# Loading the first four chunks of an attention stage as two pairs

## The chip, the cores and the metric

The kernel runs on one core of a Trainium2 chip. Its time is the device time in microseconds (us) of one execution; lower is better. Before the change five executions took 206.04 to 207.04 us, with a median of 206.45 us. One more execution was recorded by the hardware profiler. It took 206.08 us, of which the recorded span, from the first instruction to the last, is 204.3 us; the other 1.8 us lie around the span.

The engines carry their profile names: PE is the matrix engine (PEld its loading of weights into the array), DVE the vector engine, ACT the scalar engine, POOL the GpSimd engine, and SP the engine whose queue issues most of the transfers. A q behind a name (SPq, POOLq) means that engine's queue.

## The reference

A gated linear attention is followed by a two-layer network with an exact GELU. For each of 4 batches and 8 heads, a 48x48 state decays by a gate and takes up an outer product at each of 768 positions:

```python
f = 1.0 / (1.0 + np.exp(-f_logit))
for t in range(S):
    state = f[:, :, t, :, None] * state + np.einsum('bhd,bhe->bhde', k[:, :, t], v[:, :, t])
    y[:, :, t] = np.einsum('bhd,bhde->bhe', q[:, :, t], state)
```

The result is brought into the form x = 3072 positions x 384 and goes through

```python
h = x @ w_in                                    # 384 x 2048
g = 0.5 * h * (1.0 + erf(h * inv_sqrt2))
return g @ w_out                                # 2048 x 384
```

All inputs are 32-bit floats. q, k, v and f_logit are laid out as batch, head, position, dimension: one position of one head is a run of 48 numbers, 192 bytes, and two neighbouring positions of a head are one run of 384 bytes.

## The kernel before

**The tiling.** The 3072 positions are 24 chunks of 128, six to a batch. A chunk passes an attention stage, which turns the recurrence into matrix products within the chunk and a state carried from chunk to chunk, and its result is copied, transposed, into a tile `xT`. Chunks form groups of 4, 2, 2, 4, 4, 4, 4 (`SIZES`, L187); when all of a group's chunks are in `xT`, the network runs on the group: `f1` (L511 to L516) multiplies by w_in, ACT applies the GELU (L519), `f2` (L530 to L533) multiplies by w_out, and a copy and a store finish each chunk.

**The attention stage of a chunk.** `chunk_in` (L315) loads its f_logit, k, q and v as four transfers on the SP queue, 192 KB each, one position per partition, so that each consists of 1024 runs of 192 bytes. `stage1` (L329) works on batches of chunks (`BATCH`, L199; one chunk at a time for the first six): exponential and logarithm on ACT (L336, L339) give the log of the gate; a product with a triangle of -1, `trin` (L349), gives running sums; two exponentials of these (`rg` L356, `gt` L352) are multiplied on DVE into the keys (`kp` L359) and the queries (`qp` L363); POOL casts the values into `vp` (L369); small products with `negcol` (L377) give the decay of the whole chunk, `gl`. `attn` (L393) transposes keys and queries (L406); copies out of the matrix memory put them into `kb`, a block form with zeros between the heads, and `qT`; products of both (L425) are masked on DVE to `am` (L429); the state is brought on (L441, L452 to L458, L464); `am` times `vp` (L477) and the old state times `qT` (L481) give the result, which a wide copy (L490) and three narrow ones (L494) bring into `xT`. All of these copies go through one helper (L219 on ACT, L221 on DVE).

**The order of the work.** Nothing is ordered at run time. A planner (`Plan`, L64 to L160) is given every operation with an engine, an estimated duration, a priority and what it depends on, places them all on estimated times, and the instructions are emitted engine by engine in that order. Each engine then executes its queue strictly in order. Some copies of the first `ALTN` chunks have a second engine among which the planner chooses; `BIAS` (L195) adds 0.8 us to the estimate wherever ACT is the alternative. `LOCK` (L192) says from which chunk on a group's first GELU and first `f1` product wait until the exponentials and running sums of the next chunks are done, so that ACT changes its function table less often.

**Loads and weights.** `ORDER` (L188) is the order in which transfers are planned: c for a chunk, W for half of w_in, O for a quarter of w_out. Weights are issued from the POOL queue, which casts them to 16 bits: `load_win` (L292) moves a half of w_in as six transfers, three of 96 rows and three of 32; `load_wout` (L297) a quarter of w_out as one. The planner's weights-first gate (L592 to L599) lets some f_logit loads wait on SP until an earlier weight has landed. While PE waits in the opening, it multiplies `trin` by itself (L587), for no result.

```python
SIZES = [4, 2, 2, 4, 4, 4, 4]
ORDER = ['c0', 'c1', 'c2', 'c3', 'O3', 'W0', 'W1', 'O1', 'c4', 'O0', 'O2']
BATCH = [1, 1, 1, 1, 1, 1, 2, 2, 2, 2, 2, 4, 2, 1, 1]
```

Of the kernel before, what the change touches and what calls it, by code (L numbers as in the profile page):

```python
# [15 lines left out]
class Ring:  # L16


    def __init__(self, bufs, make=None, fixed=None):
        self.bufs, self.make, self.fixed, self.order = bufs, make, fixed, []  # L20
# [5 lines left out]
class Buf:  # L26
# [3 lines left out]
    def ready(self):  # L30

        r = self.ring
        if self.slot is not None or len(r.order) < r.bufs:
            return 0.0
        old = r.order[len(r.order) - r.bufs]
        t = 0.0
        for u in old.users:
            if u.end is None:
                return None
            t = max(t, u.vis)  # L40
        return t
# [15 lines left out]
JITTER = 2.0  # L57


class Op:  # L60
    __slots__ = ("eng", "dur", "fn", "bufs", "prio", "deps", "table", "start", "end", "vis", "seq", "name", "alt", "nb")


class Plan:  # L64


    def __init__(self, seed=0, bias=0.0):
        self.ops, self.w, self.r = [], {}, {}
        self.rnd, self.bias = random.Random(seed) if seed else None, bias

    def add(self, eng, dur, fn, rd=(), wr=(), bufs=(), prio=0.0, deps=(), table=None, name="", alt=None):
        o = Op()
        o.alt, o.nb = alt, 0.0
        o.eng, o.dur, o.fn, o.bufs, o.prio, o.table, o.name = eng, dur, fn, tuple(bufs), prio, table, name
# [24 lines left out]
    def run(self):  # L99
        free = {e: 0.0 for e in LAT}  # L100
        if self.rnd:
            for o in self.ops:
                o.prio += self.rnd.uniform(-JITTER, JITTER)
        act = None
# [7 lines left out]
        while left:  # L112
            best, stay, cand = None, None, []
            for o in left:
# [10 lines left out]
                for eng, dur in ((o.eng, o.dur),) if not o.alt else ((o.eng, o.dur), o.alt):  # L125
# [7 lines left out]
            for t, o, eng, dur in cand:  # L133
                if o.table and act and o.table != act and stay is not None and stay < t + 2 * SWITCH:
                    continue
                key = (int((t + (self.bias if o.alt and eng == "ACT" else 0)) * 20 + 0.999), o.prio, o.seq, t + dur)
# [9 lines left out]
            o.vis = o.end + LAT[o.eng]  # L146
# [17 lines left out]
def kernel(  # L164
# [23 lines left out]
    ORDER = ['c0', 'c1', 'c2', 'c3', 'O3', 'W0', 'W1', 'O1', 'c4', 'O0', 'O2']  # L188
    EARLY = 1.5
    WARM, FILL = 26.0, 0.75  # L190
    RMAJOR = 0
    LOCK = 12  # L192
    KBALT = 1
    ALTN = 6
    BIAS = 0.8  # L195
    SEED = 0
    CRING = 1
    HPB, ASB = 3, 3
    BATCH = [1, 1, 1, 1, 1, 1, 2, 2, 2, 2, 2, 4, 2, 1, 1]  # L199
# [5 lines left out]
    ld = ctx.enter_context(tc.tile_pool(name="ld", bufs=8))  # L205
# [8 lines left out]

    P = Plan(SEED, BIAS)

# [10 lines left out]
    negcol = one.tile([C, 1], BF16, name="negcol")  # L227

# [4 lines left out]


    NLF, NQ = 2, 4
# [3 lines left out]
    vps = [one.tile([C, H * VB], BF16, name=f"vp{i}") for i in range(NQ)]  # L239
    kbs = [one.tile([C, P2, 2, C], BF16, name=f"kb{i}") for i in range(2)]  # L240
# [12 lines left out]

    P.add("POOL", 0.5, lambda: make_identity(nc, ident), wr=["ident"], prio=-90)
    P.add("POOL", 0.5, lambda: tri(trin, -1.0), wr=["trin"], prio=-100)
    P.add("POOL", 0.5, zpad(lfs[0]), wr=["lfz0"], prio=-99)
    P.add("DVE", 0.65, zall(vps[0]), wr=["vpz0"], prio=-99)
    P.add("POOL", 0.5, lambda: tri(mask, 1.0), wr=["mask"], prio=-80)
    P.add("POOL", 0.1, lambda: nc.gpsimd.memset(negcol, -1.0), wr=["negcol"], prio=-80)
    for i in range(NQ):  # L260
        P.add("POOL", 0.2, zpad(qps[i]), wr=[f"qpz{i}"], prio=-95 + 10 * i)
        P.add("POOL", 0.2, zpad(kps[i]), wr=[f"kpz{i}"], prio=-95 + 10 * i)
        if i:
            P.add("DVE", 0.65, zall(vps[i]), wr=[f"vpz{i}"], prio=-94 + 10 * i)
    for i in range(2):
        P.add("DVE", 0.5, zall(kbs[i]), wr=[f"kbz{i}"], prio=-93 + 10 * i)
        P.add("DVE", 0.3, zall(sbs[i]), wr=[f"sbz{i}"], prio=-92 + 10 * i)
        if i:
            P.add("POOL", 0.5, zpad(lfs[i]), wr=[f"lfz{i}"], prio=-60)
# [3 lines left out]
    r_in = {n: Ring(8, lambda n=n: ld.tile([C, H, D], F32, name=n)) for n in ("qt", "kt", "vt")}  # L273
    r_lf = Ring(NLF, fixed=lfs)
    r_qp, r_kp, r_vp = Ring(NQ, fixed=qps), Ring(NQ, fixed=kps), Ring(NQ, fixed=vps)
# [3 lines left out]
    r_kb, r_sb = Ring(2, fixed=kbs), Ring(2, fixed=sbs)  # L279
    r_qT = Ring(3, lambda: at.tile([C, P2, C], BF16, name="qT"))  # L280
    r_am = Ring(3, lambda: at.tile([C, 4, C], BF16, name="am"))
# [10 lines left out]
    def load_win(kk, half, ch):  # L292
        p0, p1, r0 = ((0, 96, 96 * kk), (96, 128, 288 + 32 * kk))[half]
        cs = slice(ch * d_ff // 2, (ch + 1) * d_ff // 2)
        return nc.gpsimd.dma_start(out=win[p0:p1, kk, cs], in_=moe_w_in[r0:r0 + p1 - p0, cs])
# [4 lines left out]

    G = [dict(xT=r_xT.new(), gT=r_gT.new()) for _ in range(NG)]
    E = [dict(fl=r_fl.new(), lf=r_lf.new(), gl=r_gl.new(), glp=(r_as if CRING else r_hp).new(), gate=[]) for _ in BATCH]
# [11 lines left out]

    def chunk_in(n, prio):  # L315
        g, j = bat[n]
        b, c = divmod(n, nC)

        def src(a):
            return a[b, :, c * C:(c + 1) * C, :].rearrange("h t d -> t h d")  # L320
        f = E[g]["fl"]
# [7 lines left out]
    def stage1(g):  # L329
# [4 lines left out]
        dl = 0.19 + 0.32 * s  # L334
        pr = 10 * efirst[g]
        P.add("ACT", dl, lambda: nc.scalar.activation(fl.t()[:, 0:s], fl.t()[:, 0:s], AF.Exp, scale=-1.0),  # L336
# [6 lines left out]
        for n in ns:  # L343
# [24 lines left out]
            def cast(x=x):  # L368
                nc.gpsimd.tensor_copy(x["vp"].t().rearrange("p (h x) -> p h x", x=VB)[:, :, 0:D], x["vt"].t())  # L369
# [23 lines left out]
    def attn(n):  # L393
# [94 lines left out]
        def cols():  # L488
            return slice(j * C, (j + 1) * C)
# [155 lines left out]
```

## Time and profile before

| what | value |
|---|---|
| median of five executions | 206.45 us (206.04 to 207.04) |
| profiled execution, and its span | 206.08 us, 204.3 us |
| first `f1` product starts | 28.74 us into the span |
| last product ends, last store is issued | 201.0 us, 201.52 us |
| busy shares: PE, PEld, DVE, ACT, POOL | 93%, 63%, 61%, 66%, 27% |
| moved by DMA | 27.02 MB; HBM read 25.17 MB, written 4.72 MB |
| loads of f_logit, k, q, v | 96 transfers of 192 KB |
| load queue (SP), weight queue (POOL) | 64.9% and 10.3% of 16 engines' span |

The first page of the profile also shows each engine's busy share in 40 equal slices of about 5.1 us, in tenths:

```profile
PE   6998769999889997997999999999999999999993
DVE  6599740039793899989998589963299862000000
```

A slice of PE marked 9 is not proof of a busy array: products overlap in the pipeline, and the opening's products on `trin` count as busy. In the DVE row the two zeros in the seventh and eighth slices are the time in which PE runs the first group's `f1`. The granted PE clock is in the top tenth in all 40 slices.

### The profile page before, as it was taken

The numbers are of one execution on the slowest core, as the hardware profiler recorded it, in microseconds if no ns is written. First come the engines' busy times: TensorE is split into PE (matmuls) and PEld (weight loads), VectorE is DVE, ScalarE is ACT, GpSimd is POOL, SyncE is SP. The second block draws the span as 40 slices with busy tenths as digits, with TensorE's granted clock in tenths as the row PEclk, the third lists the DMA queues.
The fourth block names the chain that finished last, engine by engine and source line by source line (L and its number), as shares of the span: only waits on it lengthen the run. The fifth ranks groups of instructions, "written<-read, shape, count | busy, mean of one in ns | idle before, by whom it ended". The sixth has DMA issues, their size and how long they took to land.

```text
span 204.3 us, 4585 instructions
## 1 busy us (share of the span) xinstructions
PE 189.6 (93%) x1746; PEld 128.1 (63%) x1746; DVE 124.1 (61%) x270; ACT 135.6 (66%) x247; POOL 54.6 (27%) x117
## 2 busy tenths in 40 slices
PE   6998769999889997997999999999999999999993
PEld 5888734456567766865666677655676655644561
DVE  6599740039793899989998589963299862000000
ACT  4445349964579597977968973878978773169410
POOL 7238990004024135312333032030042200000000
PEclk9999999999999999999999999999999999999999
DMA  7999999999999999998999999400121000220022
GB/s 130 187 177 162 180 161 174 187 198 247 205 201 187 172 229 192 171 196 197 203 187 169 188 177 242 97 0 2 42 77 39 3 0 0 80 77 0 0 77 77
DMA packets 106388, 27.02 MB, mean 132 GB/s; under 512 B 100480, under 2 KB 105600, under 8 KB 106368
## 3 DMA queue, kind: packets, MB, share of 16 engines
q1 hardware_dynamic: 103296, 23.60, 64.9%
q0 software_dynamic: 3072, 3.15, 10.3%
q8 instruction: 13, 0.21, 0.5%
q14 instruction: 7, 0.06, 0.1%
HBM read 25.17 MB, written 4.72 MB: 146 GB/s over the span
## 4 chain that ended last, share of the span: by engine, by line
PE 67%; DVE 10%; SPq 8%; DMA 6%; issue 4%; ACT 2%; POOL 1%; DVEq 0%; ACTq 0%; POOLq 0%
PE hps L532 26%; PE hps L515 24%; SPq L326 7%; PE aps L477 4%; DMA fl<-in_f_logit_dram 4%; PE tp L406 4%; PE aps L425 3%; DVE xT L221 3%; DVE am L429 3%; DMA vt<-in_v_dram 2%; PE aps L481 2%; DVE qp L363 2%; PE aps L441 1%; PE aps L349 1%; DVE kb L221 1%
## 5 line engine op out<-in xcount | busy, mean ns | idle before, releaser
L515 PE MATMUL hps<-xT,win 128*128 128x512 bf16 (+1 forms) x336 | 69.0, 349 | 1.9 <-DVE xT L221 1.7
L532 PE MATMUL hps<-wout,gT 128*128 128x384 bf16 x384 | 68.2, 326 | 0.0
L519 ACT ACTIVATE gT<-hps 128x512 bf16<-128x512 f32 x96 | 56.4, 597 | 12.8 <-PE hps L515 9.9
L532 PEld LDWEIGHTS <-gT 128*128 128x128 bf16 x384 | 36.4, 98 | 21.9
L515 PEld LDWEIGHTS <-win 128*128 128x128 bf16 x336 | 31.5, 98 | 25.7 <-issue 2.8
L221 DVE CAST xT<-aps 96x384 bf16<-96x384 f32 (+1 forms) x92 | 32.7, 355 | 9.2 <-PE aps L481 6.0
L429 DVE TENSOR_TENSOR am<-aps,mask 128x512 bf16<-128x512 f32 x48 | 31.0, 685 | 6.5 <-PE aps L425 6.1
L369 POOL CAST vp<-vt 128x384 bf16<-128x384 f32 x24 | 12.7, 529 | 62.4 <-DMA vt<-in_v_dram 37.7
L477 PE MATMUL aps<-am,vp 128*128 128x128 bf16 x192 | 19.8, 219 | 3.0 <-DVE am L429 2.6
L458 POOL TENSOR_TENSOR tn<-rr,gl 128x384 f32<-128x384 f32 x16 | 13.5, 845 | 29.6 <-DVE rr L456 23.3
L219 ACT ACTIVATE osb<-hps 128x384 f32<-128x384 f32 x18 | 8.8, 489 | 18.2 <-PE hps L532 18.0
L477 PEld LDWEIGHTS <-vp 128*128 128x128 bf16 x192 | 15.5, 98 | 8.6 <-issue 3.6
L359 DVE TENSOR_TENSOR kp<-kt,rg 128x384 bf16<-128x384 f32 x24 | 14.2, 590 | 10.5 <-ACT rg L356 10.2
L464 POOL CAST sb<-tn 48x192 bf16<-48x192 f32 x40 | 15.9, 397 | 12.3 <-PE aps L477 3.9
L221 DVE COPY kb<-tp 48x512 bf16<-48x512 bf16 x42 | 17.5, 418 | 0.6
L336 ACT ACTIVATE fl<-fl 128x384 f32<-128x384 f32 (+2 forms) x15 | 10.7, 715 | 10.1 <-DMA fl<-in_f_logit_dram 10.0
L356 ACT ACTIVATE rg<-aps 128x384 f32<-128x384 f32 x24 | 11.8, 491 | 7.3 <-PE aps L349 6.2
L604 ACT ACT_TABLE_LOAD x12 | 15.4, 1283 | 0.9 <-PEq L629 0.7
L587 PE MATMUL hps<-trin 128*128 128x128 bf16 x170 | 14.4, 247 | 1.4 <-POOL trin L231 1.4
L481 PE MATMUL aps<-qT,sb 128*128 128x128 bf16 x80 | 15.1, 219 | 0.0
L425 PE MATMUL aps<-qT,kb 128*128 128x128 bf16 x192 | 14.9, 219 | 0.0
L363 DVE TENSOR_TENSOR qp<-qt,gt 128x384 bf16<-128x384 f32 x24 | 14.7, 612 | 0.2
(42 smaller groups left out, 171.4 us busy)
## 6 DMA issues: line engine op xcount, KB each, us to landing
fl<-in_f_logit_dram SPq DMA_DIRECT2D x24, 192.0 KB, 4.5
kt<-in_k_dram SPq DMA_DIRECT2D x24, 192.0 KB, 4.4
qt<-in_q_dram SPq DMA_DIRECT2D x24, 192.0 KB, 4.5
vt<-in_v_dram SPq DMA_DIRECT2D x24, 192.0 KB, 4.4
out_dram<-osb SPq DMA_DIRECT2D x24, 192.0 KB, 2.1
wout<-in_moe_w_out_dram POOLq DMA_DIRECT2D x4, 384.0 KB, 7.7
win<-in_moe_w_in_dram POOLq DMA_DIRECT2D x6, 192.0 KB, 5.0
win<-in_moe_w_in_dram POOLq DMA_DIRECT2D x6, 64.0 KB, 4.4
```

Source lines behind the costliest of these rows:

```text
L221: nc.vector.tensor_copy(dst, src)
L363: P.add("DVE", 0.57, lambda x=x, gt=gt: nc.vector.tensor_tensor(x["qp"].t()[:, :, 0:D], x["qt"].t(), gt.t(), ALU.mult), rd=[("gt", n), ("q ...
L425: nc.tensor.matmul(ap_.t()[:, i * C:(i + 1) * C], kb.t()[:, p, hh, :], qT.t()[:, p, :], start=True, stop=True)
L429: P.add("DVE", 0.69, lambda ap_=ap_, am=am: nc.vector.tensor_tensor(am.t(), ap_.t().rearrange("p (h t) -> p h t", t=C), mask.unsqueeze(1). ...
L464: nc.gpsimd.tensor_copy(sb.t()[64 * hh:64 * hh + D, :, D * hh:D * hh + D], tn.t()[64 * hh:64 * hh + D, :, D * hh:D * hh + D])
L477: nc.tensor.matmul(yp.t()[:, p * C:(p + 1) * C], vwin(vp.t(), 2 * p + hh), ams[half].t()[:, 2 * (p % 2) + hh, :], start=(hh == 0), stop=(h ...
L481: nc.tensor.matmul(yp.t()[:, p * C:(p + 1) * C], osb.t()[:, p, :], qT.t()[:, p, :], start=False, stop=True)
L515: nc.tensor.matmul(hps.t()[:, i * tok:(i + 1) * tok], win[:, kk, fo * 128:(fo + 1) * 128], xT.t()[:, kk, 0:tok], start=(kk == 0), stop=(kk ...
L519: acts.append(P.add("ACT", 0.6, lambda u=u, hps=hps: nc.scalar.activation(view()[:, u * pk:(u + 1) * pk, :].rearrange("p a b -> p (a b)"), ...
L532: nc.tensor.matmul(op.t()[:, 0:d_model], view()[:, fo, s_ * C:(s_ + 1) * C], wout[:, fo, :], start=(fo == 0), stop=(fo == FO - 1))
L587: nc.tensor.matmul(buf.t()[:, 0:C], trin, trin, start=True, stop=True)
L604: nc.scalar.preload_act_table_set("natural_log_exp_and_others" if table == "exp" else "gelu_and_others")
```

## The change

The first four chunks (`2 * NDB`, NDB = 2) are loaded as pairs. Partition p holds positions 2p and 2p+1 of a 256-position pair, so that a pair's f_logit, k, q and v are four transfers of 384 KB, each of 1024 runs of 384 bytes. Within the pair a "chunk" becomes the even or the odd positions:

- running sums take two products each, with two new triangles (`trin2`), as do the sums for `gl` (`neg2`);
- the values are cast twice per chunk, each time one half of the partitions into a buffer whose other half stays zero, and `kb` is twice as wide with zero padding, so that the scores and results of each half come from two accumulated products per block; the mask is replaced by four half-wide pieces (`mask2`);
- the copies into `xT` put the positions back into order with a stride of two.

The pieces of w_in become quarters (`NW = 4`), each in two transfers of 96 and 32 partitions over all three blocks (before: halves in six transfers). A weight's issue on POOL now waits until a load `AHEAD = 4` transfers before it in the order has landed. The order of transfers, the batches, `LOCK`, `ALTN`, `BIAS` and the priorities (a table `PRI` in place of none) change, as do ring sizes: inputs 8 to 6 (plus 2 pairs), `vp` 4 to 6, `kb` 2 to 3, `am` 3 to 5. The diff, cut to its core:

```diff
-    ORDER = ['c0', 'c1', 'c2', 'c3', 'O3', 'W0', 'W1', 'O1', 'c4', 'O0', 'O2']
+    ORDER = ['c0', 'c1', 'W0', 'c2', 'c3', 'W1', 'c4', 'W2', 'c5', 'c6', 'W3', 'O0', 'O1', 'O2', 'O3']
+    AHEAD = 4
+    NW = 4
-    LOCK = 12
+    LOCK = 4
-    ALTN = 6
-    BIAS = 0.8
+    ALTN = 4
+    BIAS = 0
+    PRI = {'F': 2, 'RG': 5, 'R': -2, 'GL': 2, 'Tk': 20, 'VC': -10, 'Y': 20, 'x': 2, 'QT': 10, 'C': -2, 'T': 2, 'O': -20, 'A': 2}
+    NDB = 2
-    BATCH = [1, 1, 1, 1, 1, 1, 2, 2, 2, 2, 2, 4, 2, 1, 1]
+    BATCH = [2, 2, 1, 1, 2, 1, 1, 2, 4, 2, 1, 1, 2, 1, 1]
...
+    def tri_half(t, strict):
+        nc.gpsimd.memset(t, 0.0)
+        nc.gpsimd.affine_select(out=t, in_=t, compare_op=ALU.is_gt, fill=-1.0,
+                                base=strict, pattern=[[-1, C]], channel_multiplier=1)
+        nc.gpsimd.memset(t[0:64, 64:C], 0.0)
...
+    def load_win(half, ch):
+        p0, p1, r0 = ((0, 96, 0), (96, 128, 288))[half]
+        cs = slice(ch * d_ff // NW, (ch + 1) * d_ff // NW)
+        src = moe_w_in[r0:r0 + KO * (p1 - p0), cs].rearrange("(k p) c -> p k c", p=p1 - p0)
+        return nc.gpsimd.dma_start(out=win[p0:p1, :, cs], in_=src)
...
+            def src2(a):
+                return a[b, :, c * C:(c + 2) * C, :].rearrange("h (p i) d -> p h (i d)", i=2)
+            P.add("DMA", 1.35, lambda: nc.sync.dma_start(
+                out=pairs(f).rearrange("p (h x) -> p h x", h=H), in_=src2(f_logit)),
...
+            def cum(gps=gps, j=j):
+                for i in range(1 + dbl):
+                    nc.tensor.matmul(gps.t()[:, 0:H * D], trin2[:, int(i > j)] if dbl else trin,
+                                     lf.t()[:, i if dbl else j, :, 0:D], start=(i == 0), stop=(i == dbl))
...
+            for a, vb in enumerate(x["vp"]):
+                rows = slice(64 * a, 64 * a + 64) if dbl else slice(0, C)
+
+                def cast(vb=vb, rows=rows, n=n):
+                    nc.gpsimd.tensor_copy(vb.t()[rows].rearrange("p (h x) -> p h x", x=VB)[:, :, 0:D],
+                                          loaded(n, "vt")[rows])
...
+                    for e in range(4):
+                        p, hh = 2 * half + e // 2, e % 2
+                        for a in range(two):
+                            nc.tensor.matmul(ap_.t()[:, e * C:(e + 1) * C], kbv(kb, a)[:, p, hh, :],
+                                             qT.t()[:, p, :, 64 * a:64 * a + 64] if dbl else qT.t()[:, p, :],
+                                             start=(a == 0), stop=(a == two - 1))
...
+    def weight(i, dur, fn, name, wr):
+        dm = [o for o in P.ops if o.home == "DMA"]
+        gate = dm[-AHEAD] if len(dm) >= AHEAD else None
+
+        def issue():
+            made[name] = r = fn()
+            if gate is not None and gate.name in made and gate.name[0] == "l":
+                wait_for(r, gate.name)
```

## The prediction

> **What bounds the kernel now.** I first read the busy time of the engines in stages that I cut where the chain of waits changes character. The columns are the stage, its length, then busy time (and instructions) of PE, PEld, DVE, ACT, POOL, the granted clock, the DMA share and GB/s.
>
> ```profile
> 16.80:28.74 11.94, 8.68 (x146) 8.12 (x146) 9.42 (x21) 5.39 (x13) 11.75 (x23) 1.00 1.10 173
> 28.74:39.10 10.36, 10.36 (x49) 4.70 (x48) 0.27 (x1) 9.69 (x16) 1.51 (x3) 1.00 1.17 178
> 39.10:60.60 21.50, 19.60 (x185) 12.98 (x184) 14.55 (x31) 13.56 (x27) 4.62 (x9) 1.00 1.12 208
> 60.60:96.30 35.70, 32.60 (x360) 25.14 (x358) 30.40 (x66) 28.35 (x52) 11.69 (x22) 1.00 1.17 192
> 96.30:128.00 31.70, 31.70 (x308) 21.27 (x306) 27.25 (x60) 24.14 (x41) 9.59 (x19) 1.00 1.17 194
> ```
>
> PE looks full, but a busy PE is no measure. So I price its products by stretches in which they run back to back, from the chain of waits (start, length, what):
>
> ```profile
> 169.76 10.40 PE hps L532 x64
> 180.16 10.36 PE hps L515 x48
> ```
>
> That is 0.1625 us for an `f2` product and 0.216 for a 512-wide `f1` product; likewise 0.108 for a 256-wide one, 0.056 for the 128-wide ones of the attention stage, 0.16 for L349. With the counts of each stage:
>
> - 39.1 to 60.6: 64 `f2` (10.4), 20 narrow `f1` (2.2), 68 attention products (3.8), the small ones 1.6: 18.0 of 21.5, so 3.5 lost.
> - 60.6 to 96.2: 10.4 + 8.5 + 161 attention products (9.0) + 3.0: 30.9 of 35.6, 4.7 lost.
> - 96.2 to 201.1: 41.5 + 41.6 + 17.9 + 3.9 = 104.9 of 104.9. Nothing is lost.
>
> Hence span = **T** (start of the first `f1`, 28.74) + 164.2 of work + **S** (8.2 lost after T) + 3.3 of copy and last store. Before T only 7.8 us of PE work is useful. Only T and S can give anything.
>
> T is set by the loads. ACT's first exponential waits for f_logit in each of the first four chunks (start, length, engine, line, what, and in brackets the idle time before):
>
> ```profile
> 3.91 0.52 ACT L336 ACTIVATE fl<-fl 128x384 f32<-128x384 f32 x1 [1.90 <-DMA fl<-in_f_logit_dram]
> 8.10 0.52 ACT L336 ACTIVATE fl<-fl 128x384 f32<-128x384 f32 x1 [1.60 <-DMA fl<-in_f_logit_dram]
> 12.29 0.52 ACT L336 ACTIVATE fl<-fl 128x384 f32<-128x384 f32 x1 [1.53 <-DMA fl<-in_f_logit_dram]
> 16.83 0.52 ACT L336 ACTIVATE fl<-fl 128x384 f32<-128x384 f32 x1 [2.11 <-DMA fl<-in_f_logit_dram]
> ```
>
> 4.2 us a chunk, so 1.05 us per transfer of 1024 short runs; f1 then starts 11.9 us after the fourth f_logit. In that time DVE is busy for 9.42 of 11.94 us: it is the next bound.
>
> **The pair loads.** 16 transfers go, 8 of double size come. The trace has no 384-byte run. If only runs count, a pair costs 1.05; if bytes count, 2.10. The second is unlikely: weights read at twice the moved bytes (read as 32 bits, written as 16), 6.29 MB in 10.3% of 204.3 us, i.e. 21 us, or 300 GB/s against 187 here. Between these ends I take a rule of the Trainium skill, "DMA: Bandwidth & Descriptors", section "How a descriptor splits into AXI transactions": a run is fetched in 32-byte beats from the 256-byte boundary below it. At 192-byte steps the runs need 6, 12, 10 and 8 beats with the unused head, 9 on average; at 384 bytes 12 and 16, so 14. With the 3 cycles per packet that its section "Why small descriptors are slow" gives, 12 against 17: 1.05 x 17/12 = 1.49 us, an estimate. The page also speaks against the change: "Specifications" asks for at least 512 bytes for line rate, and 384 is still below. By that rule alone, priced by bytes, the sum is 8 x 2.1 = 16.8 us, no saving; by the estimate it is 11.9, **4.9 us saved** of DMA time. I take 1.5.
>
> **When things land.** First f_logit pair: 3.91 + 0.45 = 4.4. The first w_in quarter now goes between the pairs: a quarter is 1/8 of the 21 us, 2.6. Second f_logit pair: 4.4 + 4 x 1.5 + 2.6 = 13.0, against 16.83 for chunk 3. Then 17.5 for its last part, W1 20.1, c4 24.3, W2 26.9, c5 31.1, c6 35.3, W3 37.9, the four O at 40.5 to 48.3. Before, all weights and c4 to c6 were in when c6's values were cast at 51.94: 3.6 later.
>
> **The stage of the pairs.** Exponential and logarithm take 0.84 each for two chunks (row 128x768) instead of 4 x 0.52: first `kp` at 4.4 + 1.7 + 0.75 (two running-sum products) + 0.52 = 7.4, 1.3 later than now (6.08). Zeroing on DVE grows: `kb` 3 x 0.96 (0.272 for 256 words, 0.485 for 512, so 0.83 ns a word for 1088) and `vp` 6 x 0.485, 6.4 with `sb` against 3.45, all before 7.4 and hidden; uncovered it would cost 3.0. PE gains 32 score and 32 result products (3.6), and 1.8 of sums: 5.4 us, beside 14.4 us of idle products; without that cover 5.4. POOL: masks and paddings 7.2 against 4.4, four more casts (2.1), but by T only some six weight issues at 0.52 instead of 16 (9.5 us with w_out): 20 of 26 us busy, as now. A weight that waits for a load has casts and state copies queued behind it on POOL; their consumers (L441, L481) have slack of some us after the second pair's f_logit, so I cost that 0, at most 2. The casts collide with DVE. Here is one (now at chunk 3):
>
> ```profile
> 20.98 0.70 DVE L363 TENSOR_TENSOR qp<-qt,gt 128x384 bf16<-128x384 f32 x1
> 21.33 0.71 POOL L369 CAST vp<-vt 128x384 bf16<-128x384 f32 x1
> ```
>
> Alone they take 0.55 and 0.50: 0.15 each. The Trainium skill, "SBUF — State Buffer", section "Who interferes with whom", has the second one blocked entirely by the first when both read that memory: up to 0.5 each. Four more casts: 0.6 by the row, 2.1 by the rule; I take the row.
>
> DVE's work before T is 22.0 - 3.45 = 18.55 us, and it needs 22.7 us for it (82%). The number of operations stays. With `BIAS` 0 ACT takes more copies: bounds 0 and 5 us (ACT has about 10 of 22 us free); I take 2.5. 18.55 - 2.5 + 0.6 = 16.65: at 82% T = 7.4 + 20.3 = 27.7, at 95% 24.9. DVE waits for four loads now and for two then, so between: **T = 26.5, 2.2 earlier**. W0 has long landed.
>
> **After T.** `f1` of the first group has its first 12 units (7.8 us) by 34.3; W3 lands at 37.9. Chunk 4's attention (1.9) lies in the gap, 1.7 lost. `f2` needs the last O at 48.3, but `f1` of group 1 (5.2) and chunks 5, 6 (3.8) fill PE until then. The 3.5 lost there before (c4 came only after all weights) become 1.7. In 60 to 96 DVE is busy for 30.4 of 35.7: loads come 3.6 earlier, but DVE stays; 4.7 becomes 3.8. **S = 5.5, 2.7 less.** `LOCK` 4 holds group 3's `f1` until the exponentials of c12 to c15, one batch (1.48 twice): c15's f_logit is issued at 85.52 and lands about 90 now, 86 then, so ready at 90; `f1` comes at 96.2 - 5 = 91. It costs 0, and each us beyond 87 costs one. Smaller input rings: loads lead by up to 6 chunks only, late in the kernel, 0. Function tables: 12 loads of 1.28 now; two more or fewer shift 2.6 us on ACT, which is 66% busy.
>
> Sum against the profiled execution: 206.08 - 2.2 - 2.7 = 201.2. Its 206.08 lies 0.37 under the median, so **201.5** by the median.
>
> **Rivals.**
> - *The loads set everything*: T = 13.0 + 11.9 = 24.9, S = 3.5: 206.45 - 3.8 - 4.7 = 198.0. For: the waits of ACT above. Against: DVE's share in the opening. 20%.
> - *The gain is given back at W3 and the last O*: PE's queue is strictly ordered, and weights now come after c6. T = 26.5, S = 10.4: 206.5. For: W3 at 37.9 against a need at 34.3. Against: group 1 can fill. 10%.
> - *Slower: DVE is the bound of the opening.* ACT takes no more copies, `kp` starts 1.3 later, and two chunks arrive at once behind wider exponentials: T = 7.4 + 19.15/0.82 = 30.8, S stays 8.2 since DVE bounds that stage too: 208.5. It decides once T exceeds 28.7. For: DVE's 9.42 of 11.94. Against: ACT is half idle there. 18%.
> - *The runs stay short or cost by bytes* (2.1 a pair): second f_logit at 5.0 + 8.4 + 2.6 = 16.0, T = 29.5, S 8.2: 207.2. Against: the two positions of a head are contiguous on both sides. 7%.
>
> My forecast has 45%; its own range is 199 to 204. The range 196 to 208.5 reaches just to the slower case. About 0.3% (0.6 us) can be told from no change. Faster 45 + 20 + some of the third; slower 18 + 6; same the rest.
>
> **What would show it.** Packets of the load queue fall by 8192; f_logit waits end near 4.4 and 13.0; the first `kp` near 7.4; the first `f1` at 25 to 28; `f1` pauses near 34 to 38; work after T still sums to 164. It is wrong if a pair needs over 1.9 us, if DVE is over 90% busy up to a T beyond 28.7, or if PE's losses after T exceed 8.

## The result, and the profile after

The changed kernel takes 204.96 us (median of 22 executions, 203.93 to 206.84); the kernel before took 206.54 us beside it (43 executions). The ratio is 0.992, with a 95% interval of 0.9902 to 0.9937: faster by 0.8%, where 2.4% was forecast. It lies in the range given (196 to 208.5), but outside that of the likeliest case (199 to 204). The profiled execution took 205.37 us, with a span of 203.6.

The busy rows of the page, to be laid beside those of before:

```profile
PE   6779696996999999987999999999999999999992
DVE  7867688350399379498999679955399870000000
```

The stretch in which DVE has little to do, the first group's `f1`, lay in the seventh to ninth slice (0, 0, 3); it now lies in the eighth to eleventh (3, 5, 0, 3). The stages of after, in the columns of the first fence of the prediction:

```profile
19.65:33.37 13.72, 10.00 (x152) 8.28 (x150) 10.66 (x24) 8.14 (x21) 9.89 (x18) 1.00 0.94 173
33.37:45.70 12.33, 12.33 (x87) 6.70 (x85) 6.52 (x15) 9.96 (x17) 4.59 (x7) 1.00 1.13 175
45.70:60.60 14.90, 12.95 (x114) 8.50 (x113) 6.33 (x13) 9.39 (x19) 2.15 (x5) 1.00 0.83 158
60.60:82.00 21.40, 21.40 (x241) 17.89 (x239) 16.62 (x39) 18.09 (x33) 7.77 (x16) 1.00 0.99 207
82.00:99.00 17.00, 14.97 (x162) 10.72 (x161) 13.31 (x28) 15.47 (x26) 3.06 (x6) 1.00 0.99 202
```

The opening now ends at 33.37, the first `f1`, where it ended at 28.74. From 60.6 to 82 PE has no gap; two stages still have some 2 us of them. Counted for both kernels alike, with the prediction's prices per product (good to some 0.4 us; the first `f1` and the losses are those of one profile each):

| term | before | forecast | after |
|---|---|---|---|
| T, first `f1` | 28.74 | 26.5 | 33.37 |
| PE work after T | 163.4 | 164.2 | 161.4 |
| S, lost after T | 8.9 | 5.5 | 5.2 |
| copy and last store | 3.3 | 3.3 | 3.6 |
| span | 204.3 | 199.5 | 203.6 |

(The prediction counted 164.2 and 8.2 before; the sum of both is nearly the same.) S ended near the forecast value; by this count it fell by 3.7 us, where 2.7 was forecast. T missed by 6.9 us, of which 2.0 came back (163.4 to 161.4), since products of chunks 4 and 5 now run ahead of the first `f1`.

The loads themselves went nearly as forecast. ACT's exponentials, in the view that the prediction showed for before:

```profile
4.30 0.84 ACT L403 ACTIVATE fl<-fl 128x768 f32<-128x768 f32 x1 [2.29 <-DMA fl<-in_f_logit_dram]
10.34 0.84 ACT L403 ACTIVATE fl<-fl 128x768 f32<-128x768 f32 x1
21.97 0.52 ACT L403 ACTIVATE fl<-fl 128x384 f32<-128x384 f32 x1
```

The second starts at 10.34, 2.7 us ahead of the forecast and 6.5 ahead of chunk 3's before; no idle time stands ahead of it, so ACT did not wait for it. The two f_logit pairs, issued at 0.74 and 4.14, landed 3.5 and 6.2 us later, so at 4.28 and 10.32: four pairs in 6.04 us, 1.51 each. From the chain of waits (start, length, what):

```profile
5.62 1.44 SPq L378
7.06 0.04 issue
7.10 1.44 SPq L378
8.54 0.04 issue
8.59 11.01 DMA vt<-in_v_dram
19.60 0.05 issue
19.65 0.50 POOL vp L449
...
20.78 1.35 POOL vp L449
...
31.75 0.83 POOL vp L449
```

SP issues a pair every 1.48 us. But the last part of the second pair, issued at 8.59, lands 11 us later: from 6.78 on, w_in quarters from POOL's queue run on the same DMA engines. The larger part of W1, issued at 10.66, lands 8.0 us later, at 18.6, ahead of values that were queued 2 us before it. The two experiments on the weights' issue below, e1 and e11, bear this out.

### The profile page after: what moved, and what is told of

It is laid out like the page before. It is cut to its first block, busy times and chain, and to the rows that moved or that the text cites. A ratio compares the mean times of both kernels' runs of the same rounds, so it can differ in the third digit from the quotient of the medians.

```text
span 203.6 us, 4638 instructions
## 1 busy us (share of the span) xinstructions
PE 188.0 (92%) x1787; PEld 128.5 (63%) x1787; DVE 122.7 (60%) x263; ACT 140.0 (69%) x257; POOL 58.0 (29%) x131
## 4 chain that ended last, share of the span: by engine, by line
PE 65%; DMA 15%; POOL 4%; SPq 4%; DVE 4%; ACT 4%; issue 3%; ACTq 0%
PE hps L681 27%; PE hps L664 23%; DMA wout<-in_moe_w_out_dram 7%; DMA vt<-in_v_dram 5%; PE aps L533 4%; PE aps L618 3%; PE tp L490 3%; SPq L378 3%; DMA fl<-in_f_logit_dram 3%; POOL vp L449 2%; PE aps L581 1%; PE aps L622 1%; PE aps L424 1%; DVE kp L435 1%; DVE am L541 1%
## 5 line engine op out<-in xcount | busy, mean ns | idle before, releaser
L668 ACT ACTIVATE gT<-hps 128x512 bf16<-128x512 f32 x96 | 56.0, 598 | 15.3 <-PE hps L664 12.5
L230 DVE CAST xT<-aps 32x128 bf16<-32x128 f32 (+1 forms) x88 | 30.9, 352 | 8.1 <-PE aps L622 4.7
L449 POOL CAST vp<-vt 128x384 bf16<-128x384 f32 (+1 forms) x28 | 15.9, 569 | 38.6 <-DMA vt<-in_v_dram 32.3
L228 ACT ACTIVATE osb<-hps 128x384 f32<-128x384 f32 x22 | 10.7, 488 | 22.7 <-PE hps L681 22.3
L439 DVE TENSOR_TENSOR qp<-qt,gt 128x384 bf16<-128x384 f32 x24 | 14.1, 589 | 18.6 <-ACT gt L428 18.5
L230 DVE COPY kb<-tp 48x512 bf16<-48x512 bf16 x45 | 18.9, 419 | 2.3 <-ACT kb L228 0.8
L604 POOL CAST sb<-tn 48x192 bf16<-48x192 f32 x40 | 14.1, 353 | 20.7 <-DVE tn L592 16.3
L618 PEld LDWEIGHTS <-vp 128*128 128x128 bf16 x224 | 17.1, 98 | 4.5 <-issue 0.9
L533 PE MATMUL aps<-qT,kb 128*128 128x128 bf16 x224 | 17.9, 219 | 1.5 <-DVE kb L230 0.9
L533 PEld LDWEIGHTS <-kb 128*128 128x128 bf16 x224 | 14.8, 98 | 5.9 <-DVE kb L230 1.4
L228 ACT ACTIVATE qT<-tp 128x512 bf16<-128x512 bf16 x23 | 13.7, 596 | 4.4 <-PE tp L490 4.3
L428 ACT ACTIVATE gt<-aps 128x384 f32<-128x384 f32 x19 | 9.4, 493 | 5.6 <-PE aps L424 5.4
```

The source lines that it names most:

```text
L228: nc.scalar.activation(dst, src, AF.Copy)
L230: nc.vector.tensor_copy(dst, src)
L449: nc.gpsimd.tensor_copy(vb.t()[rows].rearrange("p (h x) -> p h x", x=VB)[:, :, 0:D], loaded(n, "vt")[rows])
L533: nc.tensor.matmul(ap_.t()[:, e * C:(e + 1) * C], kbv(kb, a)[:, p, hh, :], qT.t()[:, p, :, 64 * a:64 * a + 64] if dbl else qT.t()[:, p, :] ...
L618: nc.tensor.matmul(yp.t()[:, p * C:(p + 1) * C], vwin(vp.t(), 2 * p + hh), ams[half][i].t()[:, 2 * (p % 2) + hh, :], start=(hh == 0 and i ...
L668: acts.append(P.add("ACT", 0.6, lambda u=u, hps=hps: nc.scalar.activation(view()[:, u * pk:(u + 1) * pk, :].rearrange("p a b -> p (a b)"), ...
```

## The experiments

All change the kernel after, and all ratios are to the kernel before, run beside them on the same chip. The changed kernel's own is 0.992 (0.9902 to 0.9937).

Times are medians of several executions, but each first `f1` is read from one profile, and PE's rate in the opening differs from profile to profile. The same 24 filler products, in the changed kernel and in e1:

```profile
7.52 1.50 PE L755 MATMUL hps<-trin 128*128 128x128 bf16 x24 [0.23 <-ACT rg L432]
8.14 2.72 PE L755 MATMUL hps<-trin 128*128 128x128 bf16 x24
```

In e1 the slow rate, there before its edit can have had an effect, lasts until some 12 us, and the first masking starts at 15.87 instead of 14.71. In eleven of the eighteen profiles the granted clock also falls in some slice of the opening or just behind it. So two first `f1` that lie within about 1 us of each other are not told apart.

### What the pairs are worth, and what they need

**e2: without pairs, the rest of the change kept** (NDB 0, batches of one for the first six chunks):

```diff
-    NDB = 2
-    CEARLY = 3
+    NDB = 0
+    CEARLY = 5
-    BATCH = [2, 2, 1, 1, 2, 1, 1, 2, 4, 2, 1, 1, 2, 1, 1]
+    BATCH = [1, 1, 1, 1, 1, 1, 2, 1, 1, 2, 4, 2, 1, 1, 2, 1, 1]
```

> NDB is 0: no chunk is loaded as a pair, the first four batches are single chunks, and the order is planned anew; the order of transfers, LOCK, ALTN, BIAS, PRI and the quarters of w_in are those of the changed kernel. Theory V and my accounting of PE's lost time (opening 2.5 us worse than before in useful work, later stages 3.8 better) say that the gain of the whole change comes from the order and not from the pairs: the time is within 1 us of the changed kernel's. The rival, that the pairs' shorter DMA time carries the gain, expects a time at or above that of the kernel before, 1.5 us or more above the changed kernel.

213.05 us, ratio 1.0291 (1.0246 to 1.0336). In this schedule, planned anew without them, the pairs are worth 8 us. Theory V, which expected a time within 1 us of the changed kernel's, missed.

**e7: pairs with the former schedule:**

```diff
-    ORDER = ['c0', 'c1', 'W0', 'c2', 'c3', 'W1', 'c4', 'W2', 'c5', 'c6', 'W3', 'O0', 'O1', 'O2', 'O3']
-    AHEAD = 4
-    NW = 4
+    ORDER = ['c0', 'c1', 'c2', 'c3', 'O3', 'W0', 'W1', 'O1', 'c4', 'O0', 'O2']
+    AHEAD = 1000
+    NW = 2
...
-    LOCK = 4
-    ALTN = 4
-    BIAS = 0
+    LOCK = 12
+    ALTN = 6
+    BIAS = 0.8
+    PRI = {}
+    BATCH = [2, 2, 1, 1, 2, 2, 2, 2, 2, 4, 2, 1, 1]
```

> The pair loads and all that they need, but with the order of transfers, the w_in halves, the ungated weights, LOCK, ALTN, BIAS, the priorities and the batches of the kernel before. Theory A (the changed schedule is the gain, and the pairs need it): time 206.5 to 209 us, the losses after the first f1 stay at 8 us. Theory P (the pairs are the gain by themselves): time 202 to 205.5 us, the second pair's f_logit lands at about 10.3, since no weight stands between the pairs. The first f1 at 30 to 33 by both.

223.38 us, ratio 1.0784 (1.0743 to 1.0826): both theories had far too little. The chain of waits of this run points to a cause:

```profile
7.31 1.44 SPq L378
8.79 21.02 DMA vt<-in_v_dram
29.86 0.08 issue
29.94 0.06 POOL vp L449
```

All weights are issued between 6.8 and 12.5 us, and the values of the second pair land 21 us after their issue. The first `f1` is at 44.8; PE's clock falls as well while it waits (last section). The next two runs test the cause.

**e11: the change without its gate:**

```diff
-    AHEAD = 4
+    AHEAD = 1000
```

> The weights' issues on POOL no longer wait for a load four places before them; order, pieces and priorities stay, the plan is made anew. Theory G (without the gate the weights share the DMA engines with the queued loads of the second pair, as in the pairs with the former schedule, where its values landed 21 us after their issue): the second pair's values land at 25 us or later, the first f1 is at 38 to 45, the time 209 to 222 us. Rival (the two transfers per piece and their place in the order suffice): time within 1 us of the changed kernel's, values at 18 to 20.5.

218.77 us, ratio 1.0596 (1.0578 to 1.0614), second values cast from 26.8, first `f1` at 46.1 (1 us past theory G's range). Theory G holds: the wait on POOL is worth nearly 14 us, the largest single piece of the change.

**e16: pairs with the new order and gate, other settings as before** (LOCK 12, ALTN 6, BIAS 0.8, no PRI, batches as in the run with the former schedule):

> The changed kernel's pairs, w_in quarters, order of transfers and gate, but LOCK 12, ALTN 6, BIAS 0.8, no priorities and batches of two as in the kernel before. Theory G (order and gate are what the pairs needed: with the former order they cost 16.6 us): second values landed by 20 us, time 204 to 206.5 us. Rival (the plan's other settings are needed as well): time 207 to 211 us.

205.67 us, ratio 0.9944 (0.9926 to 0.9962), inside theory G's range. Order, quarters and gate bring 17.7 us of the 18.4 that lie between the former schedule and the changed kernel; for the other settings no gain can be told, since the intervals overlap. In this profile the first `f1` is at 32.0, earlier than the changed kernel's, and 7.3 us are lost after it.

Neither half of the change works alone: 1.029 without the pairs, 1.078 with the former schedule, 0.992 together.

### What was tried first: loads, casts and PE

**e1: W1 issued behind the second pair's casts:**

```diff
+    late = [o for o in P.placed if o.name in ("wwin10", "wwin11")]
+    P.placed = [o for o in P.placed if o not in late]
+    last = max(i for i, o in enumerate(P.placed) if o.name == "VC3")
+    P.placed[last + 1:last + 1] = late
```

> The order of all engines is that of the changed kernel; only the two transfers of W1 (second quarter of w_in) are issued on POOL behind the casts of the second pair instead of before them. Theory V (the second pair's values, landing at 19.65 us because weight transfers share the DMA engines with them, set the opening): v lands 2 to 2.6 us earlier, near 17, its casts end near 20 instead of 22.7, the first f1 product starts 1 to 2.5 us earlier than 33.37, and the time falls by 0.5 to 2 us against the changed kernel. Theory D (DVE's and ACT's work bounds the opening whenever the data come): v lands earlier too, but the first f1 product stays within 0.7 us of 33.4 and the time within 0.5 us. W1 itself is not needed before some 36 us under both.

205.76 us, ratio 0.994 (0.9914 to 0.9965). The casts start 1.75 us earlier, at 17.9. The time did not fall. The first `f1`, at 33.9, says little: the slow rate of PE shown above had put the first pair 1.2 us behind in this profile, and DVE's wait for the second casts shrinks from 1.0 to 0.2 us.

**e3: values before queries within each pair:**

```diff
+    where = {o.name: i for i, o in enumerate(P.placed)}
+    for n in (0, 2):
+        a, b = where[f"ldqt{n}"], where[f"ldvt{n}"]
+        P.placed[a], P.placed[b] = P.placed[b], P.placed[a]
```

> The order of all engines is kept; only in each pair's four transfers v is issued before q. Theory V: v of the second pair lands about 1.5 to 3 us earlier (near 17), q later by as much; POOL's casts and the state product behind them in PE's queue come earlier, while queries have slack of some us: the first f1 product comes 0.5 to 2 us earlier and the time falls by 0.3 to 1.5 us. Theory D: within 0.5 us, or slower by up to 1 us where the queries' product on DVE now waits for q.

205.2 us, ratio 0.9921 (0.9894 to 0.9948): no change that can be told. Casts from 17.1, but DVE then waits 1.2 us for the second pair's queries, which land at 19.7; the first `f1` is at 34.5.

**e8: the second cast of each chunk copies one head of eight** (the values of the other seven are left out there):

```diff
+                    hs = slice(0, 1 if dbl and rows.start else H)
-                    nc.gpsimd.tensor_copy(vb.t()[rows].rearrange("p (h x) -> p h x", x=VB)[:, :, 0:D],
-                                          loaded(n, "vt")[rows])
+                    nc.gpsimd.tensor_copy(vb.t()[rows].rearrange("p (h x) -> p h x", x=VB)[:, hs, 0:D],
+                                          loaded(n, "vt")[rows][:, hs])
```

> In each of the first four chunks the second cast of the values (partitions 64 to 127) copies one head only: the values of the other seven heads are left out there. The order of all instructions is that of the changed kernel. Theory C (four casts in a row on POOL, 3.0 us in the trace, stand in the chain to the first f1 and shift it): two of the four casts at 19.65 shrink from 0.5 and more to about 0.1 to 0.2, the first f1 comes 1.0 to 1.5 us earlier, time 203.3 to 204.3 us. Rival (the casts' delay is absorbed by DVE's queue behind them): the first f1 within 0.4 us of 33.4 and the time within 0.4 us of the changed kernel's.

205.15 us, ratio 0.9907 (0.9876 to 0.9939): no change that can be told; first `f1` at 33.8, with the granted clock at 0.72 between 20 and 26 us.

**e9: half of the pairs' products:**

```diff
-                for i in range(1 + dbl):
+                for i in range(1):
...
-                        for a in range(two):
+                        for a in range(1):
...
-                        for i, vp in enumerate(vps_):
+                        for i, vp in enumerate(vps_[:1]):
```

> In the first four chunks the second of every two accumulated products is left out (running sums, decay, scores, state and result: 5.4 us of PE work at the rates of the trace), so that only part of each pair's sums is computed. The order of all instructions is that of the changed kernel. Forecast's step (the extra products lie beside idle time of the opening and cost nothing): time within 0.5 us of the changed kernel's, the first f1 at 33 to 34. Rival E (they stand in the chain of each pair, one behind another, and take back what the loads gave): the first f1 comes 3 to 5 us earlier, the time is 200 to 202.5 us.

204.44 us, ratio 0.9905 (0.9884 to 0.9927), which overlaps with the changed kernel's; first `f1` at 32.45: 0.9 us earlier for 5.4 us of work left out, a little more than expected (the granted clock was 0.80 between 20 and 26 us). The extra products are hidden for the most part, as forecast.

**e6: more filler products on PE:**

```diff
-    WARM, FILL = 26.0, 0.75
+    WARM, FILL = 40.0, 0.9
```

> Products on the triangle fill PE's planned gaps up to 40 us instead of 26, and 0.9 of each gap instead of 0.75. Theory K (PE at a lowered rate in the opening is part of the late first f1: its transposes take 0.63 instead of 0.39 in some of the runs): time 203.5 to 204.3 us, the first f1 about 1 us earlier, four transposes at 0.39 to 0.46 throughout the opening. Rival (the opening hangs on DVE, POOL and ACT, PE only follows): no change within 0.4 us, or slower by up to 1 us where a filler runs over a product that has become ready.

206.94 us, ratio 0.9998 (0.9981 to 1.0014). The first `f1` is at 33.2, the time 2 us longer, so the fillers gain nothing. The granted clock is in the top tenth throughout, but so it is in the changed kernel's own profile; what a faster PE would be worth in the opening is not shown. In the profiles, 1.4 us more are lost after the first `f1`, 0.9 of them between 60 and 80; why was not settled.

### What holds the opening: DVE's queue

**e10: the maskings of the first four chunks done twice:**

```diff
+                    for _ in range(1 + dbl):
-                    nc.vector.tensor_tensor(am.t(), ap_.t().rearrange("p (h t) -> p h t", t=C),
+                        nc.vector.tensor_tensor(am.t(), ap_.t().rearrange("p (h t) -> p h t", t=C),
```

> Each of the eight maskings of the first four chunks is done twice on DVE: 8 x 0.62 to 0.69, about 5.2 us more on DVE before the first f1, everything else in the changed kernel's order. Theory D (DVE's queue is the bound of the pair stage): the first f1 comes 4 to 5.5 us later, the time is 208.5 to 210.5 us. Rival (the stage is held by latencies between engines and by loads, DVE has slack there): the first f1 at most 2 us later and the time at most 207 us.

208.86 us, ratio 1.0108 (1.0093 to 1.0123). In the timeline of DVE both groups have doubled from 2.48 (start, length, engine, line, what):

```profile
15.20 5.38 DVE L542 TENSOR_TENSOR am<-aps,mask 128x512 bf16<-128x512 f32 x8 [0.54 <-PE aps L533]
...
27.87 5.37 DVE L542 TENSOR_TENSOR am<-aps,mask 128x512 bf16<-128x512 f32 x8
```

5.8 us more on DVE put the first `f1` at 38.96, 5.6 us later, and the time 3.9 us up. In this stage DVE has no slack. (That less work on DVE brings as much is a different claim; e13 to e15 test it.) What its 25.5 us from the first `kp` to T are made of shows in its groups, here of the changed kernel between 7.9 and 33.37 (busy, mean ns, then the idle time before them and what ended it):

```profile
L435 DVE TENSOR_TENSOR kp<-kt,rg 128x384 bf16<-128x384 f32 x6 | 3.4, 563 | 0.0
...
L230 DVE COPY kb<-tp 48x512 bf16<-48x512 bf16 x7 | 3.0, 421 | 0.9 <-ACT kb L228 0.8
L596 DVE TENSOR_TENSOR rr<-aps,tn 128x384 f32<-128x384 f32 x4 | 2.2, 558 | 1.2 <-POOL vp L449 1.0
L230 DVE CAST xT<-aps 32x128 bf16<-32x128 f32 x7 | 2.1, 301 | 2.1 <-ACT xT L228 2.1
L230 DVE CAST xT<-aps 96x384 bf16<-96x384 f32 x1 | 0.6, 585 | 0.0
```

Six `kp`, where four chunks need four, and two of the seven `kb` copies are chunk 4's: work of chunks 4 and 5 is in front of T. What DVE waits for in this time (total, times, longest):

```profile
DVE xT L230 <- ACT xT L228: 2.1, 5, 0.7
DVE am L541 <- POOL tn L598: 1.0, 1, 1.0
DVE rr L596 <- POOL vp L449: 1.0, 1, 1.0
DVE kb L230 <- ACT kb L228: 0.8, 2, 0.4
DVE tn L592 <- PE aps L581: 0.4, 1, 0.4
```

The second row names the wrong engine: POOL's operation ends at 14.73, when the masking has begun (14.71), and in e1, e3 and e10 the same masking waits for PE's scores (L533). The first and fourth say that each hand-over of a copy between ACT and DVE costs idle time. The last stretch of the timeline shows the foreign work and the hand-overs:

```profile
27.71 0.55 DVE L435 TENSOR_TENSOR kp<-kt,rg 128x384 bf16<-128x384 f32 x1
28.18 0.55 DVE L439 TENSOR_TENSOR qp<-qt,gt 128x384 bf16<-128x384 f32 x1
28.65 0.58 DVE L230 CAST xT<-aps 96x384 bf16<-96x384 f32 x1
29.92 0.30 DVE L230 CAST xT<-aps 32x128 bf16<-32x128 f32 x1 [0.69 <-ACT xT L228]
30.25 0.56 DVE L596 TENSOR_TENSOR rr<-aps,tn 128x384 f32<-128x384 f32 x1
30.73 0.86 DVE L230 COPY kb<-tp 48x512 bf16<-48x512 bf16 x2
31.62 0.60 DVE L435 TENSOR_TENSOR kp<-kt,rg 128x384 bf16<-128x384 f32 x1
32.25 0.30 DVE L230 CAST xT<-aps 32x128 bf16<-32x128 f32 x1
32.93 0.30 DVE L230 CAST xT<-aps 32x128 bf16<-32x128 f32 x1 [0.37 <-ACT xT L228]
```

**e5: no copy with a second engine:**

```diff
-    ALTN = 4
+    ALTN = 0
```

> No copy has a second engine any more (ALTN 0): the key blocks and the copies into xT of the first four chunks all go to DVE, the queries' copies all to ACT, and the order is planned anew. Theory H (handing the copies of one tile back and forth between ACT and DVE, each waiting for the other's last one, holds the opening; the trace has gaps of 0.3 to 1.6 us at such changes): the gaps go, the first f1 comes at 31 to 32.5 instead of 33.4, the time is 203 to 204.3 us. Theory D (the sum of DVE's work is what holds the opening, ACT's share of it is needed): DVE gets some 4 us more before the first f1, which comes at 35 to 37, the time is 206 to 208.

211.29 us, ratio 1.0196 (1.0146 to 1.0246), first `f1` at 35.4: some help of ACT is needed. The plan was made anew, and much of the loss comes after 60 us, so the size isn't DVE's alone.

**e13: chunks 4 and 5 behind the last copies:**

```diff
+    late = {"KP4": "x3", "QP4": "x3", "S4": "F1.0.1", "Tk4": "F1.0.1", "Tq4": "F1.0.1", "KP5": "F1.0.3", "QP5": "F1.0.3",
+            "A4": "F1.0.5", "S5": "F1.0.8", "Tk5": "F1.0.8", "Tq5": "F1.0.8", "Y4": "F1.0.8", "A5": "F1.0.11"}
+    for o in P.placed:
+        if o.name in late:
+            place[id(o)] = max(place[id(o)], spot[late[o.name]] + 0.3)
+        for d in o.deps:
+            place[id(o)] = max(place[id(o)], place[id(d)] + 0.001)
+    P.placed.sort(key=lambda o: place[id(o)])
```

> Same plan and engines; only the keys, queries and state of chunks 4 and 5 (on DVE about 2.9 us ahead of chunk 3's last copies into xT: 2 x 0.47, 0.48, 0.89, 0.60) are placed behind these copies, and their products between the f1 products of the first group. Theory Q (that work stands in the way on DVE; beside the f1 products DVE would have time for it): the first f1 at 30.5 to 31.5 us instead of 33.4, time 202.5 to 204 us. Rival (the work is only moved on, and PE waits for chunks 4 and 5 at group 1 instead): the first f1 as early, but the losses after it grow by as much, time within 0.6 us of the changed kernel's.

204.32 us, ratio 0.9864 (0.9842 to 0.9886). The first `f1` is at 31.8, the gain against the changed kernel 0.6% by the ratios and 0.3% by the medians. Between the theories: 1.3 us of PE's work went behind T with the rest.

**e14: all copies into xT of the first four chunks on ACT:**

```diff
+    for o in P.placed:
+        if o.name in ("X0", "x0", "X1", "x1", "X2", "x2", "X3", "x3"):
+            o.eng = "ACT"
```

> Same order; all 16 copies of the first four chunks into xT run on ACT, so that none waits for another engine's copy into the same tile. Theory H (the hand-overs, 0.3 to 0.4 us each and some 3 us in all, hold DVE's queue): DVE loses some 2.5 us of work and its gaps there, the first f1 comes at 31 to 32.3 us, time 203 to 204.2 us. Rival (ACT now needs 0.5 + 3 x 0.3 = 1.4 us a chunk in a row and is late with the queries' copies): the first f1 at 33 or later, time within 0.5 us of the changed kernel's, or above.

204.69 us, ratio 0.9891 (0.9862 to 0.9921), which overlaps with the changed kernel's; first `f1` at 32.3. DVE has 2.7 us less to do and no wait on `xT`, but T gains only 1.0. Its two longest waits between 8 and 33.4 us (total, times, longest):

```profile
DVE kb L230 <- ACT kb L228: 2.4, 2, 2.0
DVE rr L596 <- POOL vp L449: 2.1, 1, 2.1
```

Of the first, 2.0 us are one wait at 9.5, behind transposes that PE ran at the slow rate in this profile. The second says what is late next: the second pair's values, 1.0 us of waiting in the changed kernel, are now 2.1.

**e15: both edits together:**

> Both edits together. If both theories hold, the first f1 comes at 29 to 30.5 us and the time is 201.5 to 203.3 us. If only the order counts, the time is that of the version with chunks 4 and 5 behind, within 0.5 us; if neither, within 0.6 us of the changed kernel's.

204.72 us, ratio 0.9892 (0.9871 to 0.9914), first `f1` at 30.8: T gains 2.5 us, the time no more than by the first edit. DVE's last work ahead of T is now done at 28.3; ACT's eight copies into `xT`, from 28.33 to 31.45, come last.

### The losses after the first f1

**e4: LOCK back to 12:**

```diff
-    LOCK = 4
+    LOCK = 12
```

> LOCK is 12 as before the change, the rest as in the changed kernel, planned anew: group 3's first f1 and GELU no longer wait for the exponentials of chunks 12 to 15. If that wait costs what PE loses between 82 and 99 us (2.4 us), the time falls by 1 to 2.4 us. If those losses come from the loads and DVE's work in that stage, or the function-table changes saved were worth as much, it is within 0.6 us or up to 1.5 us slower.

204.7 us, ratio 0.9892 (0.9855 to 0.9929), which overlaps with that of the changed kernel; the loss between 80 and 100 us stays (2.4 against 2.3). LOCK costs nothing that can be told.

**e12: chunks 12 to 15 in two batches** (BATCH with 2, 2 for the 4):

> The exponentials of chunks 12 to 15, one batch of four, become two batches of two. Theory B (the 2.3 us that PE loses between 82 and 99 us are the wait for the fourth f_logit and for exponentials of four chunks at once): most of the loss goes, 1 to 2 us, time 203 to 204 us. Rival (the smaller batch costs a change of the function tables or the loss only moves on): time 204.5 to 206.5 us, 12 to 14 table loads.

205.84 us, ratio 0.9958 (0.9932 to 0.9984); 3.6 us are lost between 80 and 100, 1.3 more. The rival holds.

**e17: e13, and three f_logit loads forward:**

```diff
+    f = [o for o in P.placed if o.name in ("ldf13", "ldf14", "ldf15")]
+    P.placed = [o for o in P.placed if o not in f]
+    i = [o.name for o in P.placed].index("ldf12") + 1
+    P.placed[i:i] = f
```

> The version with chunks 4 and 5 behind, and on SP the f_logit loads of chunks 13 to 15 right behind that of chunk 12, ahead of the keys, queries and values of 12 to 14. Theory L (the 2.3 us lost between 82 and 99 us come from chunk 15's f_logit, which sits on SP behind loads that wait for free slots and lands at 87.6): the batch's exponential starts at 84.5 to 85.5, 1.5 to 2.3 us of the loss go, time 202 to 203.3 us. Rival (the wait is replaced by DVE's work on four chunks, or by later keys and values): the exponential as early, the loss still above 1.5 us, time 203.8 to 204.8 us.

204.3 us, ratio 0.9898 (0.9868 to 0.9927), no change against e13 that can be told. The exponential of four chunks starts at 86.97 instead of 87.61, and some 2 us are still lost. ACT's queue reaches it no earlier: no wait stands ahead of it any more.

**e18: e17, and chunk 7's loads behind the last w_out quarter:**

```diff
+    c7 = [o for o in P.placed if o.name in ("ldkt7", "ldqt7", "ldvt7")]
+    P.placed = [o for o in P.placed if o not in c7]
+    i = [o.name for o in P.placed].index("wwout3") + 1
+    P.placed[i:i] = c7
+    gates["ldkt7"] = "wout3"
```

> As the run before, and chunk 7's keys, queries and values wait on SP until the last quarter of w_out has landed. Theory O (the second group's wait for w_out, 1.1 us in two places near 48 and 50.8 us, comes from chunk 7's loads on the same DMA engines): the last quarter lands 2 to 3 us earlier, PE has no wait for w_out, time another 0.7 to 1.2 us lower. Rival (chunk 7 is then late itself): the wait moves to chunk 7's values, time the same within 0.4 us or higher.

202.71 us, ratio 0.9821 (0.9783 to 0.9858): the fastest version, 1.8% under the kernel before and 1.0% under the changed one. Of this, 0.8% is the last step, from e17. In the changed kernel, PE's queue shows two waits for w_out:

```profile
48.17 2.11 PE L681 MATMUL hps<-wout,gT 128*128 128x384 bf16 x12 [0.97 <-DMA wout<-in_moe_w_out_dram]
...
51.26 1.46 PE L681 MATMUL hps<-wout,gT 128*128 128x384 bf16 x8 [0.98 <-DMA wout<-in_moe_w_out_dram]
```

In e17 they are 0.8 us together; here neither is left. The last quarter lands 3.1 us earlier than in e17 (47.5 instead of 50.6), the median time to landing falls from 8.5 to 6.3 us, and chunk 7's values, cast 9.2 us later (52.15 instead of 42.90), are still in time. Theory O holds.

## Why the prediction was wrong in size

**Right:** the pair's price. 1.49 us was the estimate from the Trainium skill ("DMA: Bandwidth & Descriptors", "How a descriptor splits into AXI transactions"); four such transfers landed in 6.04 us, 1.51 each. The load queue's packets fell by 8,320 (8,192 forecast). The first f_logit wait ended at 4.30 (4.4). The extra products are hidden but for 0.9 us (e9). `LOCK` costs nothing that can be told. S is 5.2 (5.5), though otherwise divided: 2.0 at w_out and 2.3 between 82 and 99, nothing at W3 and nothing from 60 to 82, where 3.8 was forecast for 60 to 96.

**Right in effect, by luck:** the casts at no cost. PE's state product does wait 2.9 us for them (L581) and DVE 1.0 behind it, so "slack of some us" was not true; but neither earlier values nor shorter casts moved the time, while DVE's queue came later still. The landings also fell otherwise than the sum had them: the second f_logit landed ahead of the first w_in quarter, at 10.3 instead of 13.0, and the second values, forecast ahead of W1, landed behind it, at 19.6 instead of 17.5.

**Wrong, and the cause of the miss:** "**T = 26.5, 2.2 earlier**". The step that failed is the pricing of DVE's queue in the opening: 16.65 us of work and 2.45 of waiting from a first `kp` at 7.4. Measured, to some tenths, since neighbouring operations overlap:

- first `kp` at 7.99: 0.6 later;
- the four chunks' own work 15.7: 0.95 less, since ACT took 2.9 us of copies (2.5 assumed) and the 0.6 for collisions did not come on DVE;
- work of chunks 4 and 5 (two `kp`, a `qp`, a state, two `kb`): 3.1, not in the forecast. Moving it behind T (e13) gave 1.6 of T;
- a last zeroing and the edge of a masking, 0.6;
- waiting 6.0, so 3.55 more: 2.9 of the 6.0 for ACT's copies into the same tiles (`xT` 2.1, `kb` 0.8), 1.0 for the values' casts, 1.6 for PE (1.0 for the first scores), the rest short pauses. The offload that the forecast counted as gain is paid with these waits; e14 took away those on `xT` and the values' wait grew.

0.6 - 0.95 + 3.1 + 0.6 + 3.55 = 6.9 us, all of the miss in T as a sum. As a cause only a part is shown: taking the foreign work and DVE's copies into `xT` away (e15) gave back 2.5 us, and then ACT's copies came last. That the offload does not pay as priced shows in e16 too: with `BIAS` 0.8 again (and the other former settings) DVE is busy for 1.1 us more, 20.6, but waits some 2.5 us less, and the first `f1` is at 32.0. The forecast asked how much work DVE keeps, and with which share it was busy before (82%); it is busy for 76% now (19.45 of 25.47), since its queue waits for other engines more. So the forecast's own sign, DVE over 90% busy, did not show although DVE's queue held the opening. The third rival named this engine and put T at 30.8; but it let S stay at 8.2, and S fell: from 60 to 80 us, where PE lost 3.0 before, it now loses nothing. T alone is also no measure of the time: e13's 1.6 us of T moved 1.3 us of PE's products behind it.

So the transfers brought what they were to bring, the opening handed it to DVE, and what remains is mainly the 3.7 us less in S, minus T's 4.6 us, of which 2.0 is work brought forward.

## What to carry to other kernels

When loads get faster, price the opening by the queue of the engine behind them, operation by operation and with what the planner puts in between, not by its former busy share; in this kernel a copy shared between two engines into one tile cost DVE 0.3 to 0.7 us of waiting at most changes. Check first what else runs on the same DMA engines: here an ungated weight queue cost 14 us, and holding back one chunk's loads for a weight that was needed earlier gave the last 1.6 us (e17 to e18). Work that overlaps a long product stage of another engine should be put into it (e13), but the gain in time is smaller than the gain in T.

## What the runs showed of the hardware

**Two kinds of queue share the DMA engines.** With all weights outstanding, a 384 KB load of 384-byte runs, issued behind seven others, landed 21.0 us after its issue; with gated weights it took 11.0.

**PE's rate differs between openings, and the row of the granted clock does not show all of it.** In the two lines at the head of the experiments 24 products take 1.50 us in one profile and 2.72 in the other, at some 8 us, and the row has its top tenth there in both. The kernel before shows the slow rate, too, until some 8 us. Later falls the row does show. The rows of the pairs with the former schedule (e7), in slices of 5.5 us; before and after had top tenths in all slices:

```profile
PE   6882529789999998998699999999999999999993
...
PEclk9999557969999999999969999999999999999998
```

PE is busy for 2, 5 and 2 tenths in the fourth to sixth slice, and the clock stands at 5, 5 and 7 in the fifth to seventh. In the profile of e13 it stands at 8 in the fifth and sixth. Whether more fillers (e6) prevent such a fall is not shown, since the changed kernel's profile has none either; they did not help the time.

**A cast on POOL stands still beside DVE.** One of four equal casts took 1.35 us instead of 0.50 (20.78 in the chain above), while DVE's `kp` and `qp` between 20.76 and 21.76 took their usual 0.54 each. It ends at 22.13, 0.37 us after DVE's second product. The cast at 31.75, which took 0.83, ends at 32.58, 0.36 after the `kp` beside it (31.62 to 32.22). So do all nine casts, in the profiles of before and after, that began while a `kp` or `qp` ran: they end 0.36 to 0.37 us after it. That is the rule of the Trainium skill that the forecast set aside ("SBUF — State Buffer", "Who interferes with whom"). The row from which it took 0.15 us for each engine fits as well: `qp` ends at 21.68, the cast at 22.04; it had caught only the end of the overlap. In the time this loss did not show (e8).
